# A recurrent attention loop: nearly all matmuls in 128-row, 32-column tiles, with four stream buffers in place of five

## The chip, the core and the metric

The kernel runs on one core of a Trainium2 chip. The core has five engines with instruction streams of their own: TensorE (PE; its weight loads are shown apart as PEld), VectorE (DVE), ScalarE (ACT), GpSimd (POOL) and SyncE (SP). SP does nothing here but issue transfers; ACT issues transfers too. The metric is the device time of one execution, in microseconds. The output must agree with the reference.

## What is computed

Two branches read the same 2048 tokens of 640 features, and a gate per token mixes them:

```python
g = sigmoid((x * gate_w).sum(-1, keepdims=True))
a = A(x, mem0, Wq, Wk, Wv, Wo, seg_len=32)   # recurrent, 32 heads of 192
b = B(x, wqkv, wo)                           # local, dilated
out = g * a + (1 - g) * b
```

Branch A is a loop that can't be run in parallel over its 64 segments, as each hands eight memory rows to the next:

```python
mem = mem0                                   # [1, 8, 640]
for s in range(64):
    h = concat([mem, x[:, 32*s:32*s+32]], 1) # 40 rows
    q, k, v = h @ Wq, h @ Wk, h @ Wv         # 32 heads, 192 each
    scores = q @ k.T * 192 ** -0.5           # mask: 8 memory columns, or causal
    o = softmax(scores) @ v
    o = o @ Wo
    mem = o[:, :8]
    outs.append(o[:, 8:])
```

The four weights of branch A are 7.9 MB each in bf16.

## The kernel before

**Stages.** Branch B runs first and leaves its scaled result in DRAM (`bsc_dram`). A pre-pass (`prepass`) computes q, k and v of the last eight tokens of each segment for all segments at once ("z rows") and leaves them in DRAM (`zpk_dram`). Then comes the loop of `part_a` (from line 528), and a last stage (`part_z`) multiplies the z rows' attention output with Wo.

**Rows of a segment.** One segment's tile `hT` (128 x 5 x 32) holds eight memory rows and 24 token rows, features on partitions. The z rows come from `zpk_dram` as q in `QTa`, k in `KTz` and v in `Vz`.

**Weights.** Each of the 80 slices is 128 x 1536 in bf16 (384 KB): five feature chunks kc for each of q, k, v and each of four head groups R, and 20 slices of Wo in two column parts ("oa", 384 columns; "ob", 256). 66 slices stay in SBUF. `weights_setup` (line 339) gives every slice a time of use from a hand-written list of gaps and picks the 14 that are streamed anew in each segment, at even distances. A streamed slice takes one of `WBUFS` = 5 rotating buffers (tile `wst`). `get_slice` issues its load on SP (line 382, or 380 for Wo's part from a scratch copy). SP's queue is in order, and a load waits until the slice five before it has been used.

**One segment on TensorE.** The order of PE, ACT and DVE in the loop is written out by hand (lines 713 to 789):

- `m_qk(i)`, line 540: q (even i) or k (odd i) of head group R = i // 2. For each chunk kc there are four matmuls with 384 moving columns. Their weights are `hT[:, kc, :]`, 32 columns; `tile_position=(0, 32*j)` places them side by side in the array, each with 128 rows and 32 columns. The accumulators come from the PSUM pool `psm` (two banks); the one of i = 1 comes from `psS` (two tiles of two banks).
- `c_qk(i)`, line 549: ACT copies the result to SBUF (DVE for i = 7).
- `t_qk(i)`, line 557: three 128x128 transposes into a tile of `psx` (two banks).
- `c_t(i)`, lines 564 and 568: DVE copies q to `QTa` or k to `KV`.
- `s_a(R)`, line 587, and `s_b(h)`, line 596: scores against the segment's keys and against the z keys. A head's 192 features are a full chunk of 128 and a half chunk. Two heads share a mixed chunk, which is done with 64-row weights (HALF); the full chunks use 128x128 weights (FULL). The result is a 128 x 448 block of which only the four 32-row diagonal blocks are wanted.
- `e_exp`, line 605: four ACT instructions, one for each diagonal block; `e_mask`, line 609, on DVE.
- `e_norm`, lines 616 to 623: row sums with a 128x128 block matrix of ones, Ln and Exp on ACT, two products on DVE.
- `m_v(R)`, line 633, and `c_v(R)`, line 640: v, in the way of `m_qk`.
- `pv_half(h)`, lines 656 and 661: P*V in tiles of 32 rows and 128 or 64 columns, and copies to SBUF (line 667; z part line 676).
- `o_group(part, i2)`, line 697: the output projection, four chunks at a time, in 128-row, 32-column tiles.
- ACT copies the result to `whi` (lines 778 and 786); `sel` (line 707) picks and transposes the memory rows with 128x128 weights, and DVE writes them into the next `hT` (line 710). Columns 0 to 383 ("oa") are selected between groups 8 and 9 of "ob", the rest (`sel_b`) in the next segment.
- `tail` (line 794) applies the gate in the next segment, `store` writes the rows, and `load_z` and `load_vz` load the next z rows on ACT's queue. POOL rearranges the z keys into `KTz` (line 514).

Of the kernel before, what the change touches and what calls it, by code (L numbers as in the profile page):

```python
# [7 lines left out]
ACT = mybir.ActivationFunctionType  # L8
# [9 lines left out]
WBUFS = 5  # L18
# [6 lines left out]
class _K:  # L25
# [295 lines left out]
    def slice_keys(self):  # L321
        keys = []
        for R in range(4):
            keys += [("q", R, kc) for kc in range(self.KC)] + [("k", R, kc) for kc in range(self.KC)]
        for R in range(4):
            keys += [("v", R, kc) for kc in range(self.KC)]
        keys += [("oa", i) for i in range(12)] + [("ob", i) for i in range(8)]
        return keys
# [10 lines left out]
    def weights_setup(self):  # L339
        nc, tc = self.nc, self.tc  # L340
        keys = self.slice_keys()
        gap = {("q", 0, 0): 300, ("k", 0, 1): 160, ("k", 0, 3): 70, ("k", 1, 0): 450, ("k", 2, 0): 850, ("k", 3, 0): 1050,
               ("v", 1, 0): 1000, ("v", 2, 0): 600, ("v", 3, 0): 570, ("v", 3, 3): 200, ("oa", 6): 1200}
        at, t = {}, 0
        for k in keys:
            t += gap.get(k, 0)
            at[k] = t
            t += 163
# [130 lines left out]
    def part_a(self):  # L479
# [4 lines left out]
        with ctx:  # L484
# [11 lines left out]
            KT = KV[:, 0:768].rearrange("p (c k) -> p c k", k=32)  # L496
# [3 lines left out]
            KTz = pers.tile([128, 12, 32], BF, name="KTz")  # L500

            psm = ctx.enter_context(tc.tile_pool(name="psm", bufs=2, space=bass.MemoryType.PSUM))
            psx = ctx.enter_context(tc.tile_pool(name="psx", bufs=2, space=bass.MemoryType.PSUM))
            psS = ctx.enter_context(tc.tile_pool(name="psS", bufs=2, space=bass.MemoryType.PSUM))
# [7 lines left out]
            def load_z(s):  # L512
                nc.scalar.dma_start(ZQ[:, 608:1376], self.zpk_dram[s, :, 384:1152])
                nc.gpsimd.tensor_copy(KTz[:].rearrange("p c (R i) -> p c R i", i=8),
                                      ZQ[:, 608:992].rearrange("p (R c i) -> p c R i", c=12, i=8))
# [12 lines left out]
            for s in range(nseg):  # L528
                pqs, sts, pTs, pSs = {}, {}, {}, {}

                def m_qk(i, kcs):
                    R, m = i // 2, ("q", "k")[i % 2]
                    if i not in pqs:
                        pqs[i] = psS.tile([128, 2, 512], F32, tag="S", name="ps_qk")[:, 0, :] if i == 1 else \
                            psm.tile([128, 512], F32, tag="m", name="ps_qk")
# [15 lines left out]
                def t_qk(i):  # L551
                    R = i // 2
                    st = sts.pop(i)
                    pT = psx.tile([128, 1024], BF, tag="x", name="ps_qkT")
                    pT = pT[:, 0:384].rearrange("p (t j b i) -> p t j b i", t=3, j=4, i=8)
# [363 lines left out]
```

## Time and profile before

| what | value |
|---|---|
| median of three runs | 1781.37 us (1781.3 to 1782.31) |
| span of the profiled execution | 1775.1 us |
| granted TensorE clock, mean over the span | 0.991 |
| HBM read, written | 421.44 MB, 35.52 MB |
| DMA share, 500 to 1700 us | 0.92, 301 GB/s |
| ACT, DVE, POOL busy, 500 to 1700 us | 627, 431, 30 of 1200 us |

The span runs from the first to the last instruction; what lies around it is not in the profile. The run times take in both, and the profiled execution is one execution beside the three that were timed.

In the views, a line of the chain gives start, length and what ran: the chain of work that ended last, followed back from the end. The timeline gives start, length, engine, line, operation, the tiles and the shape (weights' rows*columns, then rows x moving columns). Matmuls overlap, and each one's shown length includes its passage through the array, so the distance from start to start tells how often one can follow another. The trace's single records give these starts in nanoseconds.

### The profile page before, as it was taken

What the parts mean: (1) busy time and instruction counts of PE and PEld (TensorE: products, weight loads), DVE (VectorE), ACT (ScalarE), POOL (GpSimd) and SP (SyncE); (2) the same over time, 40 slices, a digit from 0 to 9 for tenths busy, and PEclk for the clock granted to TensorE, in tenths of its full rate; (3) what the DMA queues carried; (4) which work ended last, traced back from release to release, by engine and by line L of the source; (5) the groups of instructions that cost most, each with busy time, mean ns of one, the idle gap of its engine ahead of it and who ended that gap; (6) DMA issues with size and microseconds to landing.
All of it is one profiled execution on the core that took longest, in us unless ns stands there. A gap on an engine that the chain in (4) does not pass through costs nothing.

```text
span 1775.1 us, 82404 instructions
## 1 busy us (share of the span) xinstructions
PE 1674.0 (94%) x36512; PEld 997.3 (56%) x36527; DVE 651.2 (37%) x2047; ACT 870.1 (49%) x2377; POOL 72.7 (4%) x151
## 2 busy tenths in 40 slices
PE   6998999887999999999999999999999999999989
PEld 3554644334565655555556555555555556555557
DVE  4556533222333333333333333333333333333320
ACT  3766622223555555555555555555545555545550
POOL 4001000002000000000000000000000000000000
PEclk9999999998999999999999999999999999999999
DMA  6610195798899999999999999999999999989981
GB/s 164 203 32 29 46 315 171 207 283 233 293 301 307 305 300 301 300 299 304 300 294 304 308 293 308 298 297 297 305 292 299 301 297 304 303 289 300 299 282 30
DMA packets 280968, 461.12 MB, mean 260 GB/s; under 512 B 97188, under 2 KB 158116, under 8 KB 280612
## 3 DMA queue, kind: packets, MB, share of 16 engines
q1 hardware_dynamic: 173464, 395.75, 67.5%
q10 hardware_dynamic: 107148, 60.12, 11.9%
q8 instruction: 285, 4.67, 1.0%
q14 instruction: 71, 0.58, 0.1%
HBM read 421.44 MB, written 35.52 MB: 257 GB/s over the span
## 4 chain that ended last, share of the span: by engine, by line
PE 84%; ACT 6%; DMA 4%; issue 3%; DVE 2%; ACTq 1%; DVEq 0%
PE ps_qk L540 25%; PE ps_v L633 13%; PE ps_wo L697 11%; PE ps_qkT L557 6%; PE ps_pre L424 6%; PE ps_S L587 5%; PE ps_oT L656 3%; PE ps_z L851 3%; PE ps_bqk L220 3%; ACT bP L243 2%; DMA zpk_dram<-ZV 2%; ACT ZQ L778 2%; PE ps_mem L707 1%; PE ps_S L596 1%; PE ps_bv L207 1%
## 5 line engine op out<-in xcount | busy, mean ns | idle before, releaser
L549 ACT CAST KV<-ps_qk 128x384 bf16<-128x384 f32 x448 | 208.7, 480 | 340.2 <-PE ps_qk L540 196.5
L540 PEld LDWEIGHTS <-hT 128*32 128x32 bf16 x10240 | 247.7, 96 | 163.8 <-issue 21.0
L540 PE MATMUL ps_qk<-wlate_k,hT 128*32 128x384 bf16 x4352 | 270.0, 329 | 2.0 <-issue 2.0
L564 DVE COPY ZQ<-ps_qkT 128x384 bf16<-128x384 bf16 x256 | 91.6, 358 | 382.4 <-PE ps_qkT L557 216.8
L633 PE MATMUL ps_v<-wlate_v,hT 128*32 128x384 bf16 x4096 | 225.3, 330 | 0.0
L605 ACT ACTIVATE ZQ<-ps_S 32x224 bf16<-32x224 f32 x512 | 178.1, 348 | 43.7 <-PE ps_S L596 38.2
L697 PEld LDWEIGHTS <-KV 128*32 128x32 bf16 x6144 | 154.3, 96 | 67.0 <-issue 19.1
L540 PE MATMUL ps_qk<-wres_q,hT 128*32 128x384 bf16 x2816 | 164.2, 330 | 11.9 <-DMA hT<-in_A_mem_dram 10.7
L540 PE MATMUL ps_qk<-wst,hT 128*32 128x384 bf16 x1792 | 154.1, 328 | 0.6 <-DMA hT<-in_A_mem_dram 0.3
L633 PEld LDWEIGHTS <-hT 128*32 128x32 bf16 x5120 | 113.6, 96 | 66.8 <-issue 4.4
L697 PE MATMUL ps_wo<-wlate_oa,KV 128*32 128x384 bf16 x2560 | 140.4, 327 | 2.0 <-DVE ZQ L676 1.0
L587 PE MATMUL ps_S<-ZQ,KV 128*128 128x160 bf16 (+1 forms) x1024 | 136.9, 238 | 0.7 <-DMA ZQ<-zpk_dram 0.7
L697 PE MATMUL ps_wo<-wlate_ob,KV 128*32 128x256 bf16 x2688 | 124.2, 275 | 7.6 <-issue 7.5
L557 PE MATMUL ps_qkT<-ident,KV 128*128 128x128 bf16 x1536 | 130.0, 220 | 0.4 <-issue 0.4
L557 PEld LDWEIGHTS <-KV 128*128 128x128 bf16 x1536 | 89.0, 98 | 61.0 <-issue 40.8
L667 DVE CAST KV<-ps_oT 128x192 bf16<-128x192 f32 x256 | 79.2, 351 | 62.7 <-PE ps_oT L661 62.7
L587 PEld LDWEIGHTS <-KV 128*128 128x128 bf16 (+1 forms) x1024 | 58.8, 95 | 69.5 <-issue 42.2
L667 ACT CAST KV<-ps_oT 128x192 bf16<-128x192 f32 x256 | 69.6, 326 | 57.3 <-PE ps_oT L661 57.3
L710 DVE CAST hT<-ps_mem 128x24 bf16<-128x24 f32 x126 | 22.5, 179 | 199.1 <-PE ps_mem L707 199.1
L640 ACT CAST KV<-ps_v 128x384 bf16<-128x384 f32 x192 | 92.4, 481 | 3.3 <-PE ps_v L633 0.2
L633 PE MATMUL ps_v<-wst,hT 128*32 128x384 bf16 x1024 | 87.1, 330 | 2.4 <-DMA wst<-in_A_Wv_dram 2.4
L568 DVE COPY KV<-ps_qkT 128x384 bf16<-128x384 bf16 x256 | 89.0, 348 | 0.6 <-PE ps_qkT L557 0.4
(135 smaller groups left out, 2262.7 us busy)
## 6 DMA issues: line engine op xcount, KB each, us to landing
wst<-in_A_Wq_dram SPq DMA_DIRECT2D x260, 384.0 KB
wst<-in_A_Wv_dram SPq DMA_DIRECT2D x260, 384.0 KB
wst<-in_A_Wk_dram SPq DMA_DIRECT2D x195, 384.0 KB
wst<-wscr SPq DMA_DIRECT2D x192, 384.0 KB
zpk_dram<-ZS ACTq DMA_DIRECT2D x4, 3072.0 KB
ZQ<-zpk_dram ACTq DMA_DIRECT2D x64, 192.0 KB
wlate_k<-in_A_Wk_dram SPq DMA_DIRECT2D x17, 384.0 KB
wlate_v<-in_A_Wv_dram SPq DMA_DIRECT2D x16, 384.0 KB
```

The lines of the kernel that those rows point to most:

```text
L424: nc.tensor.matmul(ps[:], lhsT=sls[kc][:, c0:c0 + 128], rhs=zT[:, kc, :], start=(kc == 0), stop=(kc == KC - 1))
L540: nc.tensor.matmul(pq[32 * j:32 * j + 32, 0:384], lhsT=hT[:, kc, :], rhs=sl[:, 384 * j:384 * j + 384], start=(kc == 0), stop=(kc == KC - 1 ...
L549: cp(sts[i], pqs[i][:, 0:384])
L557: nc.tensor.transpose(pT[:, t, :, :, :].rearrange("p j b i -> p (j b i)"), st[:, 128 * t:128 * t + 128], self.ident[:])
L564: nc.vector.tensor_copy(q_blocks(R)[:, 1:5, :, :].rearrange("p b c i -> p c b i"), pT.rearrange("p t j b i -> p (t j) b i"))
L568: nc.vector.tensor_copy(KV[:, 384 * (R % 2):384 * (R % 2) + 384], pT.rearrange("p t j b i -> p (t j b i)"))
L587: nc.tensor.matmul(grid(h, par)[:, :, 0:80].rearrange("p j (b r i) -> p j b r i", r=2, i=8)[:, :, :, r, :], lhsT=KT[k0:k1, 12 * r + c:12 * ...
L605: nc.scalar.activation(E[ps], pSs[h][ps, :, 112 * j:112 * j + 112], ACT.Exp, scale=scale_a)
L633: nc.tensor.matmul(pvs[R][32 * j:32 * j + 32, 0:384], lhsT=hT[:, kc, :], rhs=sl[:, 384 * j:384 * j + 384], start=(kc == 0), stop=(kc == KC ...
L640: cp(V[R], pvs[R][:, 0:384])
L667: cps[j % 2](oTxs[2 * h + j // 2][:, 6 * (j % 2):6 * (j % 2) + 6, :], pos[j][:, 0:240].rearrange("p (c q) -> p c q", q=40)[:, :, 8:40])
L697: nc.tensor.matmul(pso[part][32 * jj:32 * jj + 32, 0:n], lhsT=oTxs[2 * (R // 2) + j // 2][:, 6 * (j % 2) + 3 * (R % 2) + t, :], rhs=o_weig ...
```

## The change

- `WBUFS` is 4, and the streamed slices are chosen by a new list in the order of use (`consume_order`) in place of `slice_keys` and the table of gaps; there are still 14 of them.
- Transposes, scores, sums and the memory selects are issued as matmuls with 128 rows and 32 columns at `tile_position=(0, 32*j)`, four side by side. Only P*V keeps its form. Three transposes become twelve, four score matmuls sixteen, two sums eight.
- Only the diagonal blocks of the scores are computed. For that, the mixed chunk of K^T is held twice in `KTh`, once with its upper and once with its lower 64 rows zero; `KTz` likewise. The zeros are written once, ahead of the loop. ACT copies one half, DVE the other.
- A score tile is now one bank: exp is one ACT instruction of 128 partitions for each half, and the sums stand behind the scores in the same bank.
- PSUM: `psm` has three banks (the accumulators of all projections), `psS` three tiles of one bank, `psx` two as before.
- The order of the loop is rewritten: three first accumulators instead of two are begun before the memory select; transposes and scores stand between chunks of the projections; five "oa" groups instead of six stand before the second P*V; the "oa" memory select stands at the end of the segment.

```diff
-WBUFS = 5
+WBUFS = 4
...
-                    for t in range(3):
-                        nc.tensor.transpose(pT[:, t, :, :, :].rearrange("p j b i -> p (j b i)"),
-                                            st[:, 128 * t:128 * t + 128], self.ident[:])
+                    for t in range(3):
+                        for cb in range(4):
+                            nc.tensor.transpose(pT[32 * cb:32 * cb + 32, t, :],
+                                                st[:, 128 * t + 32 * cb:128 * t + 32 * cb + 32], self.ident[:],
+                                                tile_position=(0, 32 * cb))
...
+                        nc.scalar.copy(KTh[64:128, r, 1, :], pT[64:128, 1, :])
+                        nc.vector.tensor_copy(KV[:, 384 * r:384 * r + 256].rearrange("p (t x) -> p t x", t=2),
+                                              pT[:, 0:3:2, :])
+                        nc.vector.tensor_copy(KTh[0:64, r, 0, :], pT[0:64, 1, :])
...
+                    kt = [KV[:, 384 * r:384 * r + 128], KV[:, 384 * r + 128:384 * r + 256], KTh[:, r, 0, :], KTh[:, r, 1, :]]
+                    for n, (t, par) in enumerate(((0, 0), (2, 1), (1, 0), (1, 1))):
+                        for j in range(4):
+                            ps = slice(32 * j, 32 * j + 32)
+                            nc.tensor.matmul(grid(h, par)[ps, 0:80].rearrange("p (b r i) -> p b r i", r=2, i=8)[:, :, r, :],
+                                             lhsT=kt[n][:, 32 * j:32 * j + 32], rhs=q_blocks(R)[:, :, 4 * t + j, :],
+                                             start=(r == 0 and n == 0), stop=False, tile_position=(0, 32 * j),
+                                             skip_group_check=True)
...
+                def e_sum(h):
+                    E, pz = Es[h], zsum(h)
+                    for f0, f1, o1 in ((0, 80, 80), (80, 112, 32)):
+                        for j in range(4):
+                            ps = slice(32 * j, 32 * j + 32)
+                            nc.tensor.matmul(pz[ps, :, 0:o1], lhsT=self.bones[:, ps], rhs=E[:, :, f0:f1],
+                                             start=(f0 == 0), stop=(f0 == 80), tile_position=(0, 32 * j),
+                                             skip_group_check=True)
...
                 m_qk(0, (0, 1, 2))
-                m_qk(1, (0, 1))
+                m_qk(1, (0, 1, 2))
                 if sel_b is not None:
                     sel_b()
-                m_qk(1, (2,))
+                m_qk(2, (0, 1, 2))
                 if tail is not None:
                     tail()
                 m_qk(0, (3, 4)); c_qk(0)
                 m_qk(1, (3, 4)); c_qk(1)
-                m_qk(2, range(KC))
-                t_qk(0); c_t(0); c_qk(2); t_qk(1); c_t(1)
-                m_qk(3, range(KC)); c_qk(3)
+                m_qk(2, (3, 4))
+                m_qk(3, (0, 1))
+                t_qk(0); c_t(0); c_qk(2)
+                m_qk(3, (2, 3, 4))
+                t_qk(1); c_qk(3); c_t(1)
...
+                m_qk(5, (1, 2, 3, 4))
+                t_qk(4); c_qk(5)
+                m_qk(6, (0,))
+                s_a(1); s_b(0); c_t(4); e_exp(0); e_mask(0)
+                m_qk(6, (1, 2, 3, 4)); c_qk(6)
+                t_qk(5); c_t(5)
+                m_qk(7)
+                e_sum(0); e_inv(0)
...
                 pos = pv_half(0)
-                m_v(3, (0, 1, 2))
+                e_sum(1); e_inv(1)
                 c_z(0, pos, (1, 3), "dd")
-                e_norm(1)
-                m_v(3, (3, 4)); c_v(3)
+                m_v(3); c_v(3)
+                e_mul(1)
                 c_z(0, pos, (0, 2), "aa")
-                for i2 in range(6):
+                for i2 in range(5):
                     o_group("oa", i2)
                 pos = pv_half(1)
                 c_z(1, pos, range(4), "adad")
...
-                for i2 in range(5):
+                o_group("oa", 5)
+                for i2 in range(6):
                     o_group("ob", i2)
                 for i2 in (6, 9, 7, 10, 8, 11):
                     o_group("oa", i2)
                 nc.scalar.copy(whi[:, 0:384], pso["oa"][:, 0:384])
                 if s + 1 < nseg:
                     load_z(s + 1)
-                    pm = psS.tile([128, 2, 512], F32, tag="S", name="ps_mem")
-                for i2 in range(5, 12):
+                for i2 in range(6, 12):
                     o_group("ob", i2)
-                    if i2 == 8 and s + 1 < nseg:
-                        sel("oa", hT_next, pm)
                 nc.scalar.copy(whi[:, 384:640], pso["ob"][:, 0:256])
                 if s + 1 < nseg:
+                    pm = psS.tile([128, 512], F32, tag="S", name="ps_mem")
+                    sel("oa", hT_next, pm)
```

## The prediction

> **What bounds the kernel now.** I read the page first (busy times, then the chain that ended last), next the chain inside one segment of the loop, then the timeline of earlier small matmuls, then two stages by window, and last the stream tile.
>
> ```profile
> PE 1674.0 (94%) x36512; PEld 997.3 (56%) x36527; DVE 651.2 (37%) x2047; ACT 870.1 (49%) x2377; POOL 72.7 (4%) x151
> PE 84%; ACT 6%; DMA 4%; issue 3%; DVE 2%; ACTq 1%; DVEq 0%
> ```
>
> TensorE sets the end. The 64 segments lie between about 430 and 1717 us. From the first gate matmul (line 794) at 432.4 us to the 63rd at 1691.5 us there are 62 periods, 20.31 us each; the shortest is 19.71. The segment from 918.25 to 938.23 us (19.98) is my model; these pieces of its chain show the pattern.
>
> ```profile
> 918.25 0.83 PE ps_qk L540 x20
> 919.08 0.14 PE ps_mem L707 x2
> 919.21 0.28 PE ps_qk L540 x4
> 919.49 0.07 PE ps_a L794 x4
> 919.56 1.57 PE ps_qk L540 x36
> 921.13 0.44 PE ps_qkT L557 x6
> 921.57 1.74 PE ps_qk L540 x40
> ...
> 937.03 0.49 ACT ZQ L778
> 937.52 0.05 issue
> 937.56 0.23 PE ps_mem L707 x3
> ```
>
> Four projection matmuls, one per 32-column tile, run side by side: 163 ns per four, start to start. So 40 of them need 1.63 us, but after six 128x128 transposes they took 1.74. In the records the first transpose starts 269 ns after the last projection four (106 more than 163), the others follow at 56 ns, and the next four starts 149 ns after the last transpose (93 more than 56, and the four behind it is 10 late). Each excursion from the 128x32 form therefore costs about 0.21 us beside its own work.
>
> ```profile
> 156.30 0.23 PE L260 MATMUL ps_bO<-bP,bV 128*32 128x121 bf16 x4
> 156.36 0.23 PE L260 MATMUL ps_bZ<-bP,b_ones 128*32 128x121 bf16 x4
> 156.41 0.22 PE L260 MATMUL ps_bO<-bP,bV 128*32 128x121 bf16 x4
> ...
> 212.58 0.22 PE L260 MATMUL ps_bZ<-bP,b_ones 63*32 63x56 bf16 x4
> 212.62 0.21 PE L260 MATMUL ps_bO<-bP,bV 63*32 63x56 bf16 x4
> ```
>
> These are small matmuls in 32-column tiles, weights changing every four: 121 columns cost 53 to 57 ns per four. For 56 columns the records have 25 to 26 ns between fours that run undisturbed (38 to 40 for the first pair).
>
> ```profile
> 918.25:938.24 19.99, 19.84 (x497) 11.92 (x493) 7.30 (x27) 10.60 (x32) 0.51 (x1) 1.00 0.92 303
> 225.00:250.00 25.00, 24.29 (x111) 11.13 (x115) 7.90 (x12) 6.52 (x12) 0.00 (x0) 1.00 0.98 363
> ```
>
> The last three columns are granted clock, DMA share and GB/s. The segment moves 303 GB/s; when loads were queued up, 363 were reached. So a segment's 6.06 MB need at least 16.7 us.
>
> ```profile
> who waited for it (us, times):
>   PE ps_v L633: 2.4, 2
>   DVE ZQ L564: 1.9, 1
> ```
>
> That is the stream tile (wst) between 500 and 1700 us: the projections hardly wait for their 14 loads per segment. In the semaphore records a load lands 4.61 us after its issue on the mean (5th, 50th, 75th, 95th percentile 3.82, 4.49, 4.97, 5.78), and it is used a median 2.3 us after that. **The slack exists because five buffers span five slices.**
>
> **What leaves.** Time of each excursion above its projections, from the chain: memory select b 0.26; transposes 0, 1: 0.56; transposes 2, 3 with scores 0: 0.87; scores 1 with transposes 4, 5: 1.05; transposes 6, 7 with scores 2 and sums: 0.97; scores 3: 0.70; sums 1: 0.33; memory select a with its wait for ACT's copy: 0.46. Sum 5.18 us. The two P*V excursions (0.58 each) stay.
>
> **What comes.** Transposes: 8 x 3 fours of 128 columns at 55 ns = 1.32. The trace has no 80-column four; between 26 ns (56 columns) and 55 ns (121) I take 37: 4 x 4 fours = 0.59 (0.42 to 0.88). Their z part has 32 columns; 25 ns, as for P*V's fours of 40 columns: 8 fours = 0.20. Sums: 160 columns 0.07 (line 794's row) and 64 columns 0.03, twice = 0.20. Selects: 5 fours at 25 ns = 0.13. Sum 2.44. The mixed chunk, padded and run twice, is in the 0.59; it replaces two half-height matmuls that ran together.
>
> **Waits that move.** The select for the first three chunks now stands at the very end, with nothing between it and the projections that read its result. In the trace the last select matmul starts at 937.63 and the first dependent projection at 938.07, 0.44 later, with three output groups of 0.11 inside. Without them the wait is 0.42. It also still waits some 0.11 for ACT's 0.48 us copy, since six groups of 0.11 follow the last 384-column group. The fourth projection needs the first one's PSUM buffer back: copy finished 0.38 + 0.48 after the last four, handoff 0.05, against 5 fours = 0.82: 0.10. Added: 0.63. Gone: the wait behind the gate matmul (0.10; select b now has 3 fours of projections as cover), 0.08 ahead of the second P*V and 0.18 behind it (six groups and one more now cover the copies, 0.82 instead of 0.55). Ahead of the second P*V ACT has two copies of 0.33, Ln and Exp of 0.31 and 0.29, and V's copy of 0.48 to do; a wait of up to 0.4 can come back there, and I take 0. TensorE's segment: 19.98 - 5.18 + 2.44 + 0.63 - 0.36 = **17.5 us**. The mean lies 0.33 above the model segment. Single stalls make that up, such as 1.1 us at 914.4, where the page names nothing but issue; a 16 KB instruction load (queue q8) had started at 913.06. Matmuls per segment go from 493 to 664, so it will hardly shrink: 17.85 on the mean.
>
> **Costed at nothing.** Exp goes from 4 instructions of 348 ns to one per half: ACT loses some 2.1 us of 10.6 and gains four copies of half-height K^T (between the rows 0.22 and 0.48, so 0.9 to 1.9). DVE's K^T copies are split (at most 4 x 0.35 more on 7.3). POOL's z copy of 0.51 becomes four, 0.5 to 2.0: it starts when the z load has landed (median 5.0 us), issued 1.2 us ahead of the segment; the first scores come 5.1 us in and the first z scores 6.3, so 0.5 us are left at the worst; without that cover it is up to 0.5 per segment. On ACT's queue the load of the local result moves behind the second exp; it is needed a quarter of a segment later at the earliest. No queue sees a new kind of load. Four buffers also serve the stages before the loop and the last one, where no more than three slices of a weight set are streamed: -5 to +5 us, 0 taken.
>
> **Four stream buffers.** The cost I do not put at nothing. A load is issued when the slice four before it has been used (45 ns after the matmuls' end). Its buffer's round is use, 0.5 us, plus landing, 4.61: four buffers feed 14 slices in 14/4 x 5.11 = 17.9 us. That is TensorE's own 17.85, and the slack, five slices of 1.45 minus 5.1, falls to about zero. Two equal limits do not give 17.9. Landings scatter by 0.6 us (half of the middle 0.8 spans 0.67 of a standard deviation); a normal scatter around zero slack is late by 0.4 x 0.6 = 0.24 on the mean, and one load in four waits afresh, since a delay also puts off the issues behind it: 3.5 x 0.24 = 0.84. **Segment: 18.75 us.** The bounds: landings of 4.0 us (loads found alone or nearly so landed in 3.4 to 4.3) leave TensorE's 17.85; landings of 5.2, if 14 slices in less time hinder each other, make 20.0.
>
> **Sum.** 63 periods x (20.31 - 18.75) = 98 us off the profiled span of 1775.1, so 1677; the median of the runs, 1781.4, lies 6.3 above that span: **1683 us**. A difference of 0.2% (3.6 us) is about what a measurement of this kernel can tell from none.
>
> **Rivals.** *TensorE alone decides* (27%). The stream is late nowhere: 1781.4 - 63 x 2.46 = 1626, up to 1650 with the 0.4 before the second P*V. For it: 363 GB/s against the 6.06 MB / 17.85 us = 339 needed. Against: five buffers' median slack of 2.3 us is less than two slices.
>
> *The ring rules outright* (18%). Landings of 5.0 to 5.3 from a DMA share already at 0.92: 19.3 to 20.3 us, so 1718 to 1781, centre 1745. For it: the loads at one place of the segment have a median of 5.4 even now. Against: fewer are in flight, and with two others in flight the median was 4.4.
>
> *The floor counts per matmul, not per four* (6%). If every matmul of the new forms needs 25 ns for itself: transposes 96 x 25 = 2.4, scores 64 x 25 = 1.6, z scores 0.8, sums 0.4, selects 0.5: 5.7 in place of 2.44. TensorE then needs 21.1, and the time is 1781 + 63 x 0.8 = 1832, **slower than before**; it decides from about 21 ns per matmul, where 228 of them take the 4.9 us that 20.31 leaves. Against: the four matmuls of 56 columns above share one 25 ns slot, with weights of their own.
> By the Trainium skill (TensorEngine Tiling (Array Packing), Instruction Overhead) each matmul has about 60 cycles of overhead, and a dimension already small should give no tiling factor; that would be this rival. The 25 ns per four in this trace do not bear it out for column tiles.
>
> *The changes of form stay in part* (4%): transposes might be set apart from matmuls of the same shape, 8 x 0.2 = 1.6 us back: some 1735. Against: between the last transpose and the scores behind it (923.5) there are 56 ns, as between two transposes.
>
> The forecast keeps 45%. Ends of the range: 1625 lets in TensorE alone, 1752 half of the ruling ring. The likeliest case's own range, landings of 4.4 to 4.8, is 1660 to 1710. Slower is the floor rival: 6%. Same is the ring's edge at 20.3 us: 1%. Faster: 93%.
>
> **What would show it.** Period of the gate matmul: 18.75 (17.9: TensorE alone; above 19.3: the ring). Transposes in three fours at 55 ns, with 163 ns to the first and no 10 ns after them. Scores' fours at 37 ns; about 0.4 us idle between the last select and the next projection. The stream tile's waits: projections late by some 0.8 us per segment, median slack under 0.5; landings near 4.6. If the period is near 17.9 and that slack stays above 1 us, the ring step is wrong; if small fours take over 80 ns, the floor is.

## The result, and the profile after

The kernel after takes 1993.4 us (median of 4 runs, 1985.5 to 2000.3); the kernel before took 1781.8 beside it (1781.3 to 1785.0). The ratio is 1.119, with a 95% interval from 1.116 to 1.123. The forecast was 1683. The profiled execution of the kernel after took 1985.5 us, its span 1983.8.

The page of the kernel after, in the rows that answer to those shown of before: busy time by engine, instruction loads of TensorE (queue q8), and the chain that ended last.

```profile
PE 1612.5 (81%) x47441; PEld 1060.3 (53%) x47456; DVE 680.0 (34%) x2303; ACT 818.2 (41%) x2249; POOL 108.3 (5%) x345
q8 instruction: 371, 6.08, 1.2%
PE 48%; issue 12%; DVE 1%; ACTq 1%; ACT 1%; DMA 1%
```

TensorE is busy for 62 us less than before, and yet the span is 209 us longer. In the chain, "issue" (time in which an engine waits for nothing that the profile shows) has gone from 3% to 12%. Queue q8 had 285 packets before and has 371 now; each carries 16 KB of instructions.

The gate matmul (line 820 now) comes every 23.65 us instead of 20.31 (62 periods each). Where that time lies shows in the chain of the kernel after, from one V projection to the next segment's first scores:

```profile
1042.24 0.15 PE ps_v L657
1042.39 1.42 issue
1043.81 0.99 PE ps_v L657 x19
...
1052.80 0.03 PE ps_qkT L570
1052.83 0.49 issue
1053.32 0.35 PE ps_qkT L570 x11
...
1054.42 0.07 ACT KV L562
...
1054.53 0.56 ACTq L830
1055.09 0.11 ACT KTh L583
...
1055.43 0.22 DVE KTh L586
...
1057.04 0.17 PE ps_qkT L570 x12
1057.21 0.65 issue
1057.86 0.34 PE ps_qk L553 x3
...
1060.68 0.17 PE ps_v L657 x4
1060.85 1.58 issue
1062.43 0.70 PE ps_v L657 x12
```

(The four pieces on ACT and DVE in between belong to a wait that is taken up further down.) The holes open in the middle of a group: after one V matmul of twenty, after one transpose of twelve. At these two places there is no data to wait for, since the next matmul reads the tiles that the one before the hole read. Nor is it the stream. The projections' waits for the stream tile between 500 and 1900 us, which were to be 0.8 us in every segment:

```profile
who waited for it (us, times):
...
  PE ps_qk L553: 1.4, 3
  PE ps_v L657: 0.6, 1
```

And the waits of TensorE's weight loads in the kernel after (line, releaser, us in total, times, longest), where line 540 of before had 21.0 us from 27 waits of this name:

```profile
PEld L553 <- issue: 85.8, 127, 10.0
PEld L721 <- issue: 69.3, 86, 3.2
PEld L680 <- issue: 60.4, 109, 2.4
```

**The holes have a place in the program, and it is counted in instructions.** TensorE's records, put in order and numbered, have 987 instructions per segment before and 1330 after (a matmul is two: its weight load and itself). Between 500 and 1900 us the kernel after has 175 steps longer than 0.7 us from one TensorE instruction to the next; 174 of them lie behind the same number modulo 256. In the kernel before it is 18 of 19. And 256 is what one q8 packet carries: 285 packets for TensorE's 73115 records before (its sequencer's 76 included), 371 for 95037 after, so 256 to 257 for each. I call each run of 256 a block, and the step from one to the next its edge. The packet starts a median of 2.1 us after TensorE has entered a block that ends in a stall, and TensorE goes on 2.4 us after the packet's start (10th to 90th percentile 2.24 to 2.68). So a block's work hides its successor's load only if it lasts longer than the two together, 4.4 to 4.5 us; I take 4.4.

Block by block, from the same records (stall: what a step at an edge has beyond 0.165 us; from edge to edge holds the rest of that step too; before is 500 to 1700 us, after 500 to 1900):

```
           blocks  work in one, mean   stall, mean   stalls in all   from edge to edge
before     228     5.12 us             0.115 us        26 us         5.26 us
after      307     3.58                0.847          260            4.56

blocks of after, by their work    stall behind them, mean   from edge to edge
2.5 to 3.0 us   (74)              1.64 us                   4.56 us
3.0 to 3.5      (94)              1.00                      4.39
3.5 to 4.0      (42)              0.50                      4.34
4.0 to 4.5      (47)              0.22                      4.60
4.5 to 5.0      (35)              0.14                      4.88
over 5.0        (10)              none                      5.68
```

Whatever a block holds, it takes 4.3 to 4.6 us, unless its work is longer.

A second, smaller loss shows in the granted clock, which is 0.991 over the span before and 0.973 after. The same stretch before and after (in the row's end: granted clock, DMA share, GB/s):

```profile
900.00:1000.00 100.00, 98.17 (x2461) 59.29 (x2457) 36.48 (x135) 52.60 (x160) 2.55 (x5) 1.00 0.92 305
```

```profile
900.00:1000.00 100.00, 81.31 (x2761) 56.57 (x2764) 31.75 (x128) 39.96 (x124) 4.20 (x16) 0.93 0.79 249
```

Between 440 and 1890 us the kernel after has 19 spells of 3.4 or 6.8 us, 72 us in all, with half the clock; the loop of before has none. Inside them four projection matmuls take 320 ns instead of 162, and TensorE's steps there come to 0.5 us per segment beyond their usual length. Each of the 19 begins 1.9 to 4.3 us after the start of a step of 1.8 us or longer; 66 steps are that long. Whether the long steps set them off was not tried.

### The profile page after: what moved, and what is told of

Same layout as the page of the kernel before. It is cut to its first block, busy times and chain, and to the rows that moved or that the text cites. A ratio compares the mean times of both kernels' runs of the same rounds, so it can differ in the third digit from the quotient of the medians.

```text
span 1983.8 us, 104774 instructions
## 1 busy us (share of the span) xinstructions
PE 1612.5 (81%) x47441; PEld 1060.3 (53%) x47456; DVE 680.0 (34%) x2303; ACT 818.2 (41%) x2249; POOL 108.3 (5%) x345
## 4 chain that ended last, share of the span: by engine, by line
PE 48%; issue 12%; DVE 1%; ACTq 1%; ACT 1%; DMA 1%
PE ps_qk L553 16%; PE ps_wo L721 10%; PE ps_v L657 8%; PE ps_qkT L570 4%; PE ps_z L877 3%; PE ps_oT L680 2%; PE ps_S L604 2%; ACTq L830 1%; PE ps_S L635 1%; PE ps_S L613 1%; PE ps_mem L732 1%; DMA wst<-in_A_Wk_dram 1%; PE ps_oT L685 1%; DVE KTh L586 1%; DVE hT L735 0%
## 5 line engine op out<-in xcount | busy, mean ns | idle before, releaser
L553 PEld LDWEIGHTS <-hT 128*32 128x32 bf16 x10240 | 261.6, 97 | 178.8 <-issue 85.8
L657 PE MATMUL ps_v<-wlate_v,hT 128*32 128x384 bf16 x4096 | 267.8, 330 | 26.8 <-issue 25.9
L570 PE MATMUL ps_qkT<-ident,KV 128*32 128x128 bf16 x6144 | 195.2, 221 | 61.0 <-issue 33.9
L721 PEld LDWEIGHTS <-KV 128*32 128x32 bf16 x6144 | 176.3, 102 | 112.1 <-issue 69.3
L553 PE MATMUL ps_qk<-wres_q,hT 128*32 128x384 bf16 x2816 | 182.3, 330 | 34.0 <-DVE hT L735 19.8
L570 PEld LDWEIGHTS <-KV 128*32 128x32 bf16 x6144 | 142.6, 97 | 117.8 <-ACT KTh L583 46.3
L721 PE MATMUL ps_wo<-wlate_oa,KV 128*32 128x384 bf16 x2816 | 170.4, 351 | 22.9 <-issue 21.3
L657 PEld LDWEIGHTS <-hT 128*32 128x32 bf16 x5120 | 136.4, 97 | 75.3 <-issue 45.8
L584 DVE COPY KV<-ps_qkT 128x256 bf16<-128x256 bf16 x256 | 74.7, 292 | 290.1 <-ACT KTh L583 289.0
L553 PE MATMUL ps_qk<-wlate_q,hT 128*32 128x384 bf16 x1536 | 113.8, 332 | 11.6 <-issue 11.6
L721 PE MATMUL ps_wo<-wlate_ob,KV 128*32 128x256 bf16 x2304 | 102.8, 288 | 19.6 <-issue 19.6
L526 POOL COPY KTz<-ZQ 128x128 bf16<-128x128 bf16 x64 | 18.5, 289 | 1420.4 <-DMA ZQ<-zpk_dram 656.5
L680 PE MATMUL ps_oT<-ZQ,KV 32*128 32x40 bf16 (+1 forms) x4096 | 70.7, 186 | 30.8 <-issue 30.1
```

The source lines that it names most:

```text
L553: nc.tensor.matmul(pq[32 * j:32 * j + 32, 0:384], lhsT=hT[:, kc, :], rhs=sl[:, 384 * j:384 * j + 384], start=(kc == 0), stop=(kc == KC - 1 ...
L570: nc.tensor.transpose(pT[32 * cb:32 * cb + 32, t, :], st[:, 128 * t + 32 * cb:128 * t + 32 * cb + 32], self.ident[:], tile_position=(0, 32 ...
L584: nc.vector.tensor_copy(KV[:, 384 * r:384 * r + 256].rearrange("p (t x) -> p t x", t=2), pT[:, 0:3:2, :])
L657: nc.tensor.matmul(pvs[R][32 * j:32 * j + 32, 0:384], lhsT=hT[:, kc, :], rhs=sl[:, 384 * j:384 * j + 384], start=(kc == 0), stop=(kc == KC ...
L680: nc.tensor.matmul(out[:, r, t, :], lhsT=V[2 * h + r][ks, f0:f1], rhs=E[ks, par, 0:80].rearrange("p (b r i) -> p b r i", r=2, i=8)[:, :, r ...
L721: nc.tensor.matmul(pso[part][32 * jj:32 * jj + 32, 0:n], lhsT=oTxs[2 * (R // 2) + j // 2][:, 6 * (j % 2) + 3 * (R % 2) + t, :], rhs=o_weig ...
```

## The experiments

Theory F (for fetch): a block cannot be had in less than its supply time, about 4.4 us; small matmuls fill blocks with less work, and the rest is stall. Its rivals at the start were S, the ring of four stream buffers (the step of the prediction that carried the largest cost), and D, waits for data in the new order. The kernel before ran beside every group of experiments and took 1773.7 to 1779.1 us there.

### More instructions alone, in the kernel before

`x1_split` cuts 43 of the 60 projection slices of the kernel before into two matmuls of 192 columns, in its old order and with its five buffers.

```
+                        cut = 2 if i > 3 or (i == 3 and kc < 3) else 1
+                        w = 384 // cut
+                        for f in range(0, 384, w):
+                            for j in range(4):
+                                nc.tensor.matmul(pq[32 * j:32 * j + 32, f:f + w], lhsT=hT[:, kc, :],
...
```

> The kernel before, with 43 of its 60 projection slices issued as two matmuls of 192 columns each instead of one of 384: the same columns are streamed, in the same order, with five buffers, and TensorE gets 1331 instructions per segment instead of 987 (the changed kernel has 1330). Theory F (instruction blocks of 256 arrive no faster than one in about 4.4 us): 1331/256 = 5.2 blocks, 22.9 us per segment or a little more, so 1945 to 1990 us, with stalls of 1 to 3 us on TensorE at every 256th instruction. Theory S (four stream buffers) and theory D (new waits in the rewritten order): neither is touched; 43 more fours at some 3 ns each, 1785 to 1800 us.

It took 1983.8 us, ratio 1.116 (1.108 to 1.123): the whole loss of the change, without any part of the change except the number of instructions. The columns are the same; TensorE's blocks hold 3.82 us instead of 5.12 and stall 0.58 us each instead of 0.115, and all 131 steps over 0.7 us lie at one number modulo 256. Spells at half the clock are 27 us here, against 72 in the kernel after, so they are not what makes the loss.

### Fewer instructions in the kernel after, and five buffers

`x2_tr128` gives the kernel after its 128x128 transposes back: 1186 instructions per segment.

```
-                        for cb in range(4):
-                            nc.tensor.transpose(pT[32 * cb:32 * cb + 32, t, :],
...
+                        nc.tensor.transpose(pT[:, t, :], st[:, 128 * t:128 * t + 128], self.ident[:])
```

> The changed kernel with its transposes as 128x128 again: 24 instead of 96 per segment, 1186 instructions instead of 1330, and eight excursions from the 128x32 form at 0.21 us come back (1.7 us). F: 4.63 blocks x 4.4 us = 20.4 us per segment at least, some blocks longer by the excursions: 21 to 21.5, so 1810 to 1860 us, faster than the changed kernel. S and D: 1.7 us more per segment, about 2090 us, slower than the changed kernel.

`x3_buf5` gives it the fifth stream buffer back (`WBUFS = 5`, and `N_STREAM = 15`, so that it fits).

> The changed kernel with five stream buffers and one more streamed slice per segment (15), so that the weights fill the same space. S: the slack of the loads returns and the segment falls by 3 us or more, below 1800 us. F and D: nothing of theirs changes: 1980 to 2005 us.

The larger transposes took 1919.2 us (ratio 1.080, 1.075 to 1.085): 74 us faster than the kernel after, though TensorE's work per segment grew. The direction is F's, the size is not: I had put the floor on the mean block, and a mean hides that dense blocks still stall (0.54 us each on the mean) while the others only got longer. The fifth buffer changed nothing: 1999.9 us, ratio 1.125 (1.117 to 1.133), stalls 267 us. **S falls with it.**

### Two of the tile forms in the kernel before

`x4_sums` makes the row sums of the second half and both memory selects in 128x32 tiles, in the kernel before.

```
+                            for j in range(4):
+                                ps = slice(32 * j, 32 * j + 32)
+                                nc.tensor.matmul(pz[ps, :, 0:o1], lhsT=self.bones[:, ps], rhs=rhs, ...
...
```

> The kernel before, with only the second half's row sums and the two memory selects in 128x32 tiles: 21 matmuls more, 1029 instructions per segment. F: 4.0 blocks x 4.4 = 17.7 us stays below TensorE's own time, so what the trace of before said of the excursions holds: 0.23 us from the sums, 0.27 from the first select, 0.05 to 0.1 from the second, 0.55 to 0.6 per segment: 1743 to 1755 us. If small matmuls in 32-column tiles were dear in themselves (25 ns each): 28 x 25 ns = 0.7 us in place of 0.2, about 1775 us.

1797.2 us, ratio 1.010 (1.007 to 1.014): slower where a gain was forecast. The stalls went from 26 to 50 us, and the gain that was to pay for them did not come. Without the edges a segment's work fell by less than 0.1 us instead of 0.55, for the drains that left had lain under waits for data. The row sums still start some 0.28 us after the matmul before them, as in the kernel before: in both they start 53 ns after the mask's end (5th to 95th percentile 53 to 54). Select a still starts some 0.41 us after, as before, since it waits for ACT's copy.

### The same loop, its edges shifted

If place counts, then instructions that do nothing useful decide by where they stand. In `x5_pad_a` and `x6_pad_b` the kernel before gets 37 weight loads more per segment, so that a segment is 1024 instructions, four blocks, and its edges fall at the same four places in every segment. The two differ only in how many such loads run once, ahead of the loop.

```
+                    for i in range(n):
+                        nc.tensor.ldweights(hT[:, 0, :], tile_position=(0, 32 * (i % 4)))
...
+                if s == 0:
+                    pad(AHEAD)
...
+                        pad(37)
                         sel("oa", hT_next, pm)
```

> The kernel before with 37 single weight loads more per segment, just ahead of the first memory select, where TensorE waits 0.41 us anyway, and 78 more once, ahead of the loop. A segment then has 1024 TensorE instructions instead of 987, four times 256, so the edges of the blocks of 256 fall at the same four places of every segment. Theory F (a block of 256 instructions cannot be had in less than about 4.4 us, the stall at its edge makes up the rest): with these 78 ahead of the loop the blocks hold 6.0, 4.7, 4.05 and 5.2 us of work, so 20.3 us per segment; 1765 to 1790 us, about the kernel before, stalls at one edge of four only. Rival (stalls have nothing to do with where the instructions lie): the same time as the other kernel of this pair.

> The same kernel as x5_pad_a with 222 single weight loads ahead of the loop instead of 78; the loop is the same instruction for instruction. Theory F: the edges now lie so that two of the four blocks hold less than 4.4 us of work, 21.6 us per segment; 1835 to 1870 us, 60 to 95 us more than x5_pad_a. Rival (stalls have nothing to do with where the instructions lie): within 5 us of x5_pad_a.

They took 1827.8 (1820.9 to 1833.4) and 1839.5 us (1835.9 to 1853.5). The first missed what F expected by 40 us; the second met its bounds, but the two lie 12 us apart where F had 60 to 95. The filling was not free: even the shortest segment has 20.50 us where before had 19.71, because the copy behind select a starts 1.06 us after that select's first matmul. Each of these weight loads raises the semaphore which that copy waits for; that this delays it was not tried by itself. So I made the pair again with small matmuls as filling.

```
+                        nc.tensor.matmul(pm[jj:jj + 32, 0, 256:264], lhsT=hT[:, 0, :], rhs=self.sel_m[:],
+                                         start=True, stop=True, tile_position=(0, jj), skip_group_check=True)
...
+                        pad(18, pm)
+                        nc.tensor.ldweights(hT[:, 0, :], tile_position=(0, 0))
```

> x5_pad_a made again with cheaper filling, since its 37 single weight loads raised a semaphore 37 times and the copy behind the memory select started 0.7 us late: now 18 small matmuls and one weight load per segment in the same place, 1024 instructions per segment, and 39 small matmuls once ahead of the loop. Theory F: the blocks hold 6.0, 4.7, 4.05 and 5.0 us of work, a stall of 0.3 to 0.5 us at one edge; 1765 to 1785 us, about the kernel before. Rival (the place of the edges is indifferent): the same time as x11_pair_b.

> The same kernel as x10_pair_a with 83 small matmuls ahead of the loop instead of 39; the loop is the same instruction for instruction. Theory F: the edges lie so that one block, around the second P*V half, holds only 3.1 us of work and waits 1.1 to 1.4 us at its end in every segment, the three others wait little; 1820 to 1845 us, 45 to 70 us more than x10_pair_a. Rival (the place of the edges is indifferent): within 5 us of x10_pair_a.

1781.9 us (ratio 1.003, 1.000 to 1.005) and 1797.1 (1.012, 1.007 to 1.016): 15 us apart, for the same loop. The sign is F's, the size a quarter to a third of it. The blocks as the records have them, two segments of each (work, then the whole step at its end if that is over 0.165 us, then how long after entering it the instruction packet started):

```
x10_pair_a   4.80 0.00 2.08 | 6.18 0.00 2.21 | 4.68 0.00 0.89 | 4.03 0.55 2.17
             4.81 0.00 2.11 | 6.18 0.00 2.70 | 4.68 0.00 1.16 | 4.03 1.14 2.73
x11_pair_b   3.07 1.11 1.77 | 4.12 0.00 1.75 | 5.89 0.00 3.24 | 6.58 0.00 2.02
             3.07 0.59 1.18 | 4.18 0.49 2.29 | 5.74 0.00 1.95 | 6.58 0.00 1.98
```

The stall comes at the end of the shortest block, always at the same instruction, in 81% of the segments of x10_pair_a and 90% of those of x11_pair_b; the block of 4.1 us behind it stalls in 41% of the latter. In the chain of x10_pair_a (first) it cuts the output projection, in that of x11_pair_b (second) the second P*V, where x10_pair_a runs through:

```profile
919.48 0.03 PE ps_oT L662 x8
919.50 1.52 PE ps_wo L698 x37
921.02 0.23 issue
921.25 0.79 PE ps_wo L698 x15
```

```profile
908.29 0.19 PE ps_oT L657 x16
908.48 0.00 PE ps_oT L662
908.48 0.93 issue
909.41 0.22 PE ps_oT L662 x7
```

The size was off because 4.4 us is no constant. The packet starts 0.9 to 3.2 us after the block is entered; a block of 3.07 us whose packet starts at 1.18 has a step of 0.59 us behind it, not 1.3. What sets that start is the next question.

### The stream beside the instruction loads

`x7_nostream` reads every streamed slice of the kernel after from a resident tile instead, `x12_halfstream` every second one, `x15_nostream_before` does to the kernel before what x7_nostream does to the kernel after.

```
-        return self.load_slice(self.wstream, key, "wst", "wst")
+        near = min((k for k in self.res_tiles if k[0] == key[0]), key=...)
+        return self.res_tiles[near]
```

> The kernel after, with every streamed weight slice of the loop read from a resident slice of the same matrix instead of loaded (this leaves out the 14 loads per segment, so the values differ). It tells whether the 4.4 us per block are the queue of instruction loads standing behind the weight stream on the DMA engines. Theory F with a fixed supply time: 1965 to 2000 us, as the kernel after. F with the supply slowed by the stream: blocks come in 3 us or less, 1690 to 1780 us. Theory S (the stream ring holds the kernel after back): 1680 to 1760 us too, but then with stalls anywhere and not at the block edges of the kernel after.

> The kernel after with every second streamed slice read from a resident slice instead (this leaves out 7 of the 14 loads per segment). Theory F with the instruction load waiting behind the weight stream: its start comes about 1.6 us after a block is entered, between the 2.1 us of the kernel after and the 1.15 us of x7_nostream, so some 4.0 us per block; 1820 to 1900 us, about half way. Rival (a full stream ring holds the kernel after back, theory S): with half the loads the ring is no bound any more; 1730 to 1760 us, as x7_nostream.

> The kernel before, with every streamed weight slice of the loop read from a resident slice of the same matrix instead of loaded (this leaves out the 14 loads per segment), as x7_nostream does to the kernel after. It is the other half of that pair: what the change is worth where instructions come in 3.5 us a block. Theory F with the supply behind the stream: the stalls at the block edges, 0.4 us per segment, nearly vanish, 19.8 to 20.0 us per segment, 1740 to 1760 us; the change is then worth about nothing (x7_nostream took 1739 us), not the 1.7 us per segment of TensorE work that it takes away, for the kernel after still stalls 74 us. Rival (the stream ring, not the instructions, holds the kernel before as well): well below, 1700 us or less.

```
                      time (ratio to before, interval)      instr.   packet's start    stalls, per   segment
                                                                     after entry       segment
x15_nostream_before   1724.7 (0.970, 0.968 to 0.972)         987     -                 0.0 us        19.73 us
before                                                       987     1.82 us           0.44          20.31
x7_nostream           1739.2 (0.980, 0.977 to 0.984)        1330     1.12              1.3           19.93
x12_halfstream        1897.7 (1.070, 1.064 to 1.075)        1330     1.64              3.2           22.11
after                 1993.4 (1.119, 1.116 to 1.123)        1330     1.96              4.4           23.65
```

(The packet's start is a mean; the few that start within 0.3 us of the entry are left out. In x15_nostream_before too few stalls mark the edges to give one.) In the kernel after with three amounts of stream, at 31, 152 and 258 GB/s of all transfers, the instruction packet starts the later, the more weights are being loaded, and the stalls follow. The 2.4 us from its start to the next instruction hardly move (2.47 in x7_nostream, 2.43 in x12_halfstream). Both times lie within F's bounds. So the supply time is about 3.6 us per block without a stream and 4.4 beside all of it. Both runs also speak against S: of the 70 steps over 0.7 us that x7_nostream still has, 67 lie at the block edge, and with half the loads a ring could hardly be full, yet 120 us of the loss stay.

x15_nostream_before fell 15 us below what F gave it. Some 16 us of its gain lie outside the 62 periods: the first gate matmul comes at 422.5 us instead of 432.4, since `get_slice` serves the pre-pass too, and what follows the 63rd is 6 us shorter. Without the stream the kernel before has hardly a stall at its edges (1.3 us in all), its period is 19.70 us in most segments, and the chain's share of issue is 1%:

```profile
PE 87%; ACT 6%; DVE 2%; DMA 2%; issue 1%; ACTq 1%; DVEq 0%
```

Even there the change is worth less than nothing, with ratios of 0.980 after and 0.970 before, since 1.3 us of stalls per segment stay after.

### TensorE's work taken away

The sharpest rival of F says that TensorE's work and waits set the time. So I took away two fifths of the projection and left the instructions: `x8_half_after` and `x9_half_before`.

```
+                            n = 384 if kc == 0 else 192
+                            nc.tensor.matmul(pq[32 * j:32 * j + 32, 0:n], lhsT=hT[:, kc, :],
+                                             rhs=sl[:, 384 * j:384 * j + n],
...
```

> The kernel after, with 192 columns instead of 384 in four of the five row chunks of every q, k and v projection (this leaves out two fifths of the projection): as many instructions as the kernel after, but 3.9 us less TensorE work per segment. Theory F: 1330 instructions are 5.2 blocks of 4.4 us, 22.9 us per segment whatever they do; 1925 to 1985 us, a gain of at most 60. Rival (TensorE's work and its waits on data set the kernel after): 23.65 less 3.9 us per segment, 1720 to 1760 us.

> The kernel before, with 192 columns instead of 384 in four of the five row chunks of every q, k and v projection (this leaves out two fifths of the projection), as x8_half_after does to the kernel after: 987 instructions per segment as before, 3.9 us less TensorE work per segment. Theory F (a block of 256 instructions takes its work or its supply, about 4.4 us, whichever is longer): 16.0 us of work become 17.5 us per segment; 1595 to 1640 us, so 300 us and more below x8_half_after, which does the same work in 1330 instructions. Rival (TensorE's work alone): 15.9 to 16.4 us per segment, 1500 to 1540 us.

x8_half_after took 1943.3 us: 3.9 us of work per segment left, 246 us in 63 segments, and the time fell by 50. A segment fell by 0.7 us, from 23.65 to 22.95. Its usual steps (the median of each, added up) fell by 3.1; against that, stalls grew by 0.9 us (1.02 per block instead of 0.85), the loss in spells at half the clock by 0.65 (215 us of such spells instead of 72), and other late steps by 0.85. So the edges took back only a part; the lower clock, 0.937 over the span, is another. The chain and the largest wait of the projections' weight loads:

```profile
PE 37%; issue 15%; DMA 5%; ACT 5%; DVE 3%; ACTq 1%; DVEq 0%
```

```profile
PEld L554 <- issue: 129.7, 161, 10.2
```

x9_half_before took 1728.6 us, above the bounds of both theories, though 215 us below x8_half_after with the same columns in fewer instructions. Its segment is 19.56 us instead of F's 17.5. The usual steps of a segment fell by 2.4 us only, not 3.9. The packet starts 2.32 us after entry instead of 1.82, the stalls grow from 0.115 to 0.4 us per block, and other waits appear, those of the row sums for the mask and of projections for a stream slice among them:

```profile
PE ps_S L617 <- DVE ZQ L610: 25.5, 46, 1.1
...
PE ps_v L635 <- DMA wst<-in_A_Wv_dram: 11.4, 22, 2.7
```

So the kernel before, with less work, becomes bound by several things at once; the kernel after stays bound by its block edges in the main.

### Smaller packets of the stream

If the instruction packet waits for stream packets ahead of it, smaller ones should let it in sooner. `x13_packets_before` and `x14_packets_after` load each slice in two transfers of half the columns.

```
+        for f0 in (0, 768):
+            self.nc.sync.dma_start(t[:, f0:f0 + 768], src[:, f0:f0 + 768])
```

> The kernel before, with every streamed slice loaded by two transfers of half its columns, so the stream's packets are 1536 bytes instead of 3072; the same bytes, the same TensorE instructions. Theory P (the instruction load waits for packets of the stream that stand ahead of it on its engine, so smaller packets let it in sooner): the mean wait from a block's start to its instruction packet falls from 1.8 toward 1.4 us, the stalls from 26 to under 15 us, 1755 to 1770 us. Rival Q (it waits for its share of a busy engine, in bytes): the wait stays at 1.8 us or above, the time within 5 us of the kernel before, or longer where the doubled transfers land later.

> The kernel after, with the same edit: two transfers of half the columns for each streamed slice, packets of 1536 bytes. Theory P (smaller packets let the instruction load in sooner): the mean wait for the packet falls from 1.96 toward 1.5 us, 5.2 blocks per segment gain 0.4 us each where they stall, 1890 to 1940 us. Rival Q (its share in bytes): 1975 to 2010 us, as the kernel after, or longer.

The wait shrinks less than P asked: before from 1.82 to 1.64 us, after from 1.96 to 1.92. The stalls fall from 26 to 11 us before, as P had it, and from 260 to 249 after. But the blocks of x13_packets_before also hold more, 5.33 us instead of 5.12, which hides more of a wait by itself. Both times contradict P: x13_packets_before took 1812.9 us (ratio 1.019, 1.016 to 1.022), x14_packets_after 1985.7 (1.116, 1.112 to 1.120, the same as the kernel after within the intervals). In the first a wait of TensorE for the mask takes the place of the stalls:

```profile
PE ps_S L622 <- DVE ZQ L615: 40.2, 51, 1.7
```

It is behind ACT's exponentials, which come late; why they do beside twice as many transfers was not followed up. So what makes the packet start late beside the stream, its place behind other packets or its share of the engines, stays open. No version faster than the kernel before was found that computes the whole.

## Why the prediction was wrong, step by step

**The step that failed** is the last one on TensorE's segment. It has the instruction load in its hand, the stall of 1.1 us at 914.4 us behind a q8 packet, and then says that the 0.33 us of single stalls "will hardly shrink", because matmuls per segment go from 493 to 664. The number that should have scaled the term stands in the same sentence. A segment has 3.9 blocks before and 5.2 after, and the work in one falls from 5.12 to 3.58 us while its supply stays at 4.4: that is a floor, not a sum of single stalls. Measured, 0.44 us per segment became 4.40 (5.2 edges of 0.847). x1_split shows that more instructions alone make a loss of the same size; x8_half_after, that of 246 us of work taken away only 50 come back as time.

Worked out from the trace of before alone, the floor would have been visible: behind 33 of its blocks lies a stall of over 0.3 us, and there the packet starts a median of 2.07 us after entry and TensorE goes on 2.40 after that. 1330 instructions are 5.2 blocks, times 4.4 us 22.9 per segment, more than the 20.31 it had. The Trainium skill (Runtime: NRT & Kernel Launch, Instruction fetch mechanics) has the block of 256 instructions and the load of the next one while the current one runs, which the trace bears out; it calls the cost of crossing a block's edge mostly hidden. The 0.85 us per edge of the kernel after contradict that.

**TensorE's own segment** was to be 17.5 us. The medians of all steps of a segment, in which stalls drop out, add to 18.2 after and 19.8 before. So 1.7 us did leave instead of 2.5; the mechanism was right and the size off by a third.

- "Time of each excursion above its projections" was taken to leave whole, 5.18 us (the eight terms add up to 5.20). For the two kinds of excursion that x4_sums changes it did not: part of the drains lay under waits for data, and these remained.
- The work that comes was about right. Transposes: 142 ns to the first four (163 expected) and 56 ns per four. Scores: 26 ns per four (37 taken). The 37 rested on a misreading: these matmuls have 40 columns, five blocks of eight, and not 80, and P*V's fours of 40 columns at 25 ns were in the trace. The idle time between the last select and the projections is 0.47 us (0.42).
- A wait was not seen: 0.8 us in four of five segments ahead of a transpose group. In the chain of the kernel after, shown above, the projection's copy on ACT (1054.42) is followed by the store that ACT issues (line 830, 0.56 us), then by the half copy of K^T (line 583), on which DVE's copies wait, and the next transposes wait for these. The prediction had counted only ACT's busy time there. The wait is as long as what is missing, 2.5 less 1.7; what it is worth by itself was not tried.

**The stream ring** was to cost 0.9 us per segment. It cost nothing that the runs show: x3_buf5 with five buffers is no faster, and the projections waited 2.0 us in all for their slices. Landings got shorter, not longer (median 4.21 us after issue, 4.49 before), since the same 14 loads have 23.6 us instead of 20.3. Since no segment came down to 18.75 us, the step was never put to the test. Where the same loads came faster, in x9_half_before with 19.56 us per segment and five buffers, the median landing was 5.1 us, and projections began to wait for slices: the 4.61 us that the sum took would hardly have held.

**The rivals.** The one on the slower side, a floor of 21 ns for every matmul, had the right shape, a price per matmul that form cannot lower, and the wrong mechanism: the fours still share 25 to 26 ns, and the price, 4.4 us for 256 instructions or 34 ns per matmul, is the supply's. It got 6%.

**The balance**, per segment: usual steps 1.7 us less; steps at the edges 4.5 us more, counted beyond their usual length (4.0 beyond 0.165 us); spells at half the clock 0.5 us more. Sum 3.3; times 63 is 208 us, where the medians of the runs are 211.6 apart. The prediction had no term for the clock.

## What to carry to other kernels

Before cutting TensorE's work into smaller tiles, count its instructions: every 256 of them need the time that their load takes beside the kernel's own transfers (here 4.4 us, 3.6 without a weight stream), and work that is shorter than that is not time won. Holes named issue in the middle of a group, at one number modulo 256, are the sign, and the cheapest test is to add instructions and take none of the work away. A small stall whose cause is known to scale with the edit belongs into the sum with that scale, not as a constant.

## What was not expected of the hardware

- The supply of instructions depends on the kernel's other transfers: in the kernel after the packet starts 1.12 us after a block is entered with no weight stream, 1.64 with half of it, 1.96 with all. In the order of before it is 1.82 beside 300 GB/s and 2.32 beside 312 (x9_half_before), so the rate of the transfers is not all that sets it. From the packet's start to the next instruction it is 2.4 to 2.5 us in all of them.
- Spells at half the clock, 3.4 or 6.8 us long, follow some of TensorE's long stalls: in the kernel after 19 of 66 steps of 1.8 us or more have one within 4.3 us of their start. The loop of before, whose longest step is 1.5 us, has none.
- No lead over the loads is saved up across several blocks. In x6_pad_b blocks of 6.05 and 6.71 us of work are followed by 3.93 and 3.14, and the short one at the end still stalls, here by 1.06 us:

```profile
906.71 0.49 ACT ZQ L785
907.20 0.05 issue
907.25 0.23 PE ps_mem L712 x3
907.48 0.44 PE ps_wo L698 x11
907.92 1.06 issue
908.98 0.27 PE ps_wo L698
```

- Where TensorE's instructions begin matters: 88 more of them ahead of the loop, which do nothing for it, move the same loop by 15 us (x10_pair_a against x11_pair_b).
